# A decode backward pass on one core: the last dK tile is stored by GpSimd over fifteen DMA engines, the two small results by SyncE

## The chip, the cores and the metric

The kernel runs on one core of a Trainium2 chip. The metric is the device time of one execution in microseconds, the median of several. A core has the engines TensorE (PE, its weight loads PEld), VectorE (DVE), ScalarE (ACT), GpSimd (POOL) and SyncE (SP), and 16 DMA engines that move data between the memory of the chip and the core's on-chip memory of 128 partitions. SyncE, ScalarE and GpSimd can issue transfers, each into a queue of its own; the same 16 DMA engines serve all queues.

## What is computed

Attention with one query per head over a context of 8192, forward and backward: 32 heads of 128 elements, bf16.

```python
def _fwd_reference(q, k, v):          # q (1,32,1,128), k and v (1,32,8192,128)
    scale = q.shape[-1] ** -0.5
    scores = jnp.einsum('bhqd,bhkd->bhqk', q, k) * scale
    attn = _softmax(scores, axis=-1)
    return jnp.einsum('bhqk,bhkd->bhqd', attn, v)

def reference(q, k, v, grad_out):
    _out, _vjp = jax.vjp(_f, q, k, v)     # _f calls _fwd_reference
    _grads = _vjp(grad_out)
    return (out, dq, dk, dv)
```

The outputs out and dq are small, 32 rows of 128 elements each. dk and dv are as large as k and v: 67 MB each. So 134 MB are read and 134 MB written.

## The kernel before, in words

**Tiles.** The work goes through 16 tiles t of two heads (HP = 16). In a tile, partition p holds 128 consecutive rows of the two heads' 16384, that is 32 KB in one piece of K and as much of V (`rows_of`, L75). A whole tile of K or V is 4 MB. Three buffers hold K tiles and two hold V tiles.

**Stages of a tile.** K is transposed by VectorE and multiplied with q by TensorE (`k_block`, L184 and L192). The scores go through max, exp and sum. V is transposed by TensorE, copied by ScalarE (L253, L259) and multiplied with grad_out (`v_scores`, L270). From the softmax p and those products come ds, the gradient at the scores. `contract` (L309) sums p times V to out and ds times K to dq on TensorE. `outer` (L329, VectorE) forms dV = p times grad_out in place over V, and dK = ds times q in place over K, each in eight parts r of 16 columns. `store` (L339) sends dV and dK to memory.

**Order.** The order of instructions on each engine is that of the program text (`manual_schedule`). The loop runs t from 0 to 16; the dK of a tile is formed one round later, as tile o = t - 1. In the last round, t = 16, only the dK of tile 15 is left: `dk(0, 2)`, `dk(2, 3)`, `dk(3, 4)` and `dk(4, 8)`, that is eight products one after the other, with a store after every second one, because tile 15 is stored in four parts (`parts`). The dK of tile 14 is stored in two halves. The dV of tile 15 is stored in four quarters too (`fine`), the one before in one piece. A quarter is 1 MB: 32 of the 128 columns of every partition, in each partition one piece of 8 KB.

**Queues.** All large loads (`load`, L81) and all stores (`store`, L339) are issued by SyncE. ScalarE issues three small transfers in all: grad_out at the start, and in `results` (L341 to L351) the two result rows out and dq from `fin_sb`. GpSimd clears buffers in the first 5 us and issues no transfer. Each transfer counts on a semaphore when it has landed; there are fewer semaphores than transfers, so they are used again, and a transfer that uses one again is issued only after the earlier transfer on it has landed.

`do_cols` (128 partitions x 2 x 32, bf16) holds the columns of grad_out. It is written once at the start, and `weights_do` (L178) reads it, last for tile 15, at about 568 us. `Kt[t]` is the K buffer of tile t, where dK stands too.

Of the kernel before, what the change touches and what calls it, by code (L numbers as in the profile page):

```python
# [15 lines left out]
NB = 8  # L16
# [11 lines left out]
def kernel(  # L28
# [11 lines left out]
    nc = tc.nc  # L40
    P = 128
    _, H, S, D = k.shape
    HP = H // 2
    NT = 2 * S // P
# [27 lines left out]
    Kt = {t: k_in[t % K_BUFS] for t in range(HP)}  # L72
    Vt = {t: v_in[t % V_BUFS] for t in range(HP)}

    def rows_of(x, t, a, b):  # L75
        return x[0, 2 * t:2 * t + 2].rearrange("h s d -> (h s) d").rearrange("(p n) d -> p n d", p=P)[:, a:b, :]
# [70 lines left out]
    do_cols = consts.tile([P, 2, H], BF16)  # L147
# [33 lines left out]
    def k_block(t, c):  # L181
        x = st[t]
        X = xkpool.tile([P, BN, NW, QD], F32, tag="XK", name="XK_sb")
        nc.vector.transpose(X[:], Kt[t][:, c * BN:(c + 1) * BN, :].rearrange("p n d -> p (n d)").bitcast(F32).rearrange(  # L184
            "p (n w j) -> p n w j", n=BN, w=NW))
        if c == 0:
            x["s"] = psS.tile([P, 512], F32, tag="s", name="s_ps")
        cols = X[:].rearrange("p n w i -> p (n w i)").bitcast(BF16).rearrange(
            "p (n w i e) -> p w e n i", n=BN, w=NW, e=2)
        for w in range(NW):  # L190
            for e2 in range(2):
                nc.tensor.matmul(x["s"][:], lhsT=q_win[:, 2 * w + e2, SL - 1 - c:SL - 1 - c + P],  # L192
                                 rhs=cols[:, w, e2], start=(c == 0 and w == 0 and e2 == 0),
                                 stop=(c == NB - 1 and w == NW - 1 and e2 == 1), skip_group_check=True)

    def s_back(t):
        x = st[t]
        x["sT"] = backs.tile([P, BN, QD], F32, tag="back", name="sT")
        nc.vector.transpose(x["sT"][:].rearrange("p n r -> p (n r)"), x.pop("s")[:])  # L199

    def s_top(t):
        x = st[t]
        mx = small.tile([P, 1], F32, tag="mx")
        nc.vector.reduce_max(mx[:], x["sT"][:, :, 0:NB], axis=AX.XY)  # L204
        top = small.tile([P, 1], F32, tag="top")
        nc.vector.tensor_scalar_mul(top[:], mx[:], scale)
        nc.tensor.transpose(x["m"][:, 128:256], top[:].to_broadcast([P, P]), ident_f[:])  # L207

    def s_exp(t):
        x = st[t]  # L210
        nbias = small.tile([P, 1], F32, tag="nbias")
        for s in range(2):
            a, b = s * HF, (s + 1) * HF
            nc.vector.tensor_reduce(nbias[a:b], x["m"][a:b, 128 + a:128 + b], axis=AX.X, op=ALU.max, negate=True)
        e = x["e"] = single.tile([P, NT], F32, tag="e", name="e")
        rs = small.tile([P, 1], F32, tag="rs")
        nc.scalar.activation(e[:].rearrange("p (c n) -> p n c", c=NB), x["sT"][:, :, 0:NB], ACT.Exp, bias=nbias[:],
                             scale=scale, accum_out=rs[:])
        return rs
# [41 lines left out]
    def v_scores(t, z):  # L261
        x = st[t]
        cols = x.pop(("XV", z)).rearrange("p m s -> p (m s)").bitcast(BF16).rearrange(
            "p (m s e) -> p e m s", s=P, e=2)
        if z == 0:
            x["dp"] = psD.tile([P, 512], F32, tag="dp", name="dp_ps")
        at = SL - 2 - 2 * z
        for e2 in range(2):
            for b in range(NQ):
                nc.tensor.matmul(x["dp"][b * QD:(b + 1) * QD, :], lhsT=do_win[:, b // 2, e2, at:at + QD],  # L270
                                 rhs=cols[:, e2, :, b * QD:(b + 1) * QD],
                                 start=(z == 0 and e2 == 0), stop=(z == NZ - 1 and e2 == 1), skip_group_check=True)
# [52 lines left out]
    def outer(t, which, r):  # L325
        x = st[t]
        X, row = (Kt[t], 0) if which == "ds" else (Vt[t], 1)
        a, b = r * BN, (r + 1) * BN
        nc.vector.tensor_tensor(  # L329
            X[:, a:b, :].rearrange("p n (a b) -> p n a b", b=R),  # L330
            x[which][:, a:b, :].unsqueeze(2).to_broadcast([P, BN, D // R, R]),
            x["qd"][:, row, :].rearrange("p (a b) -> p a b", b=R).unsqueeze(1).to_broadcast([P, BN, D // R, R]),
            op=ALU.mult)

    def store(t, which, parts=1, last=None):
        X, dst = (Kt[t], out_2) if which == "ds" else (Vt[t], out_3)
        L = NT // parts
        for c in (range(parts) if last is None else (last,)):
            nc.sync.dma_start(rows_of(dst, t, c * L, (c + 1) * L), X[:, c * L:(c + 1) * L, :])  # L339

    def results():  # L341
        half = single.tile([P, 2, H], BF16, tag="ds1", name="half")
        nc.scalar.copy(half[:, 0], o_all[:])
        nc.scalar.copy(half[:, 1], dq_all[:])
        fin_ps = psT.tile([P, 2 * TB, P], BF16, tag="T", name="fin_ps")
        for i in range(2):
            nc.tensor.transpose(fin_ps[0:H, i, :], half[:, i], ident[:])
        fin_sb = small.tile([H, 2, D], BF16, tag="qd", name="fin_sb")
        nc.scalar.copy(fin_sb[:], fin_ps[0:H, 0:2, :])
        for i, dst in enumerate((out_0, out_1)):  # L350
            nc.scalar.dma_start(dst.rearrange("b h s d -> (b h s) d"), fin_sb[:, i])  # L351

    NV = NZ * NM // TB

    def v_part(t, m):
        v_bank(t, m)
        v_copy(t, m)
# [18 lines left out]
    for t in range(HP + 1):  # L376
        o = t - 1
        now, old = t < HP, t > 0
        parts = 4 if o == HP - 1 else 2 if o == HP - 2 else 1

        def dk(a, b):
            for r in range(a, b if old else a):
                outer(o, "ds", r)
                if (r + 1) % (NB // parts) == 0:
                    store(o, "ds", parts, r * parts // NB)

        dk(0, 2)
        if now:
            if old:
                v_part(t, 3)  # L390
                v_part(t, 4)
            s_back(t)
            s_top(t)
            if old:
                v_scores(t, 0)
                v_part(t, 5)
                v_part(t, 6)
        dk(2, 3)
        if now:
            rs = s_exp(t)  # L400
            if old:
                for m in (7, 8, 9):
                    v_bank(t, m)
            s_sum(t, rs)
            if old:
                v_copy(t, 7)
                v_copy(t, 8)
        dk(3, 4)
        if now:
            p_of(t)  # L410
            if old:
                v_copy(t, 9)
                v_scores(t, 1)
                v_part(t, 10)
                v_part(t, 11)
                contract(t, "p")
                v_part(t, 12)
                v_part(t, 13)
                v_scores(t, 2)
                v_part(t, 14)  # L420
                v_part(t, 15)
                v_scores(t, 3)
            else:
                contract(t, "p")
            if old and t + 1 < HP:
                weights_do(t + 1)
        dk(4, NB)
        if not now:
            break
        fine = t == 0 or t == HP - 1  # L430
        outer(t, "p", 0)
        outer(t, "p", 1)
        if fine:
            store(t, "p", 4, 0)
        v_back(t)
        pd_sum(t)
        if t % ST == 0 and old:
            gather(o, "ds")
        outer(t, "p", 2)
        ds_of(t)  # L440
        contract(t, "ds")
        if t % ST == ST - 1:
            gather(t, "p")
        if t + 1 < HP:
            prepare(t + 1)
        else:
            gather(t, "ds")
        for r in range(3, NB):
            outer(t, "p", r)
            if fine and r % 2:  # L450
                store(t, "p", 4, r // 2)
            if t + 1 < HP and t != 1 and r >= HALF - 1:
                k_block(t + 1, r - HALF + 1)
        if not fine:
            store(t, "p")
        if t == 1:
            for c in range(HALF + 1):
                k_block(t + 1, c)
        if t + 1 < HP:
            for c in range(HALF + 1, NB):  # L460
                k_block(t + 1, c)
                v_part(t + 1, c - HALF - 1)
            if t + 2 < HP:
                weights_q(t + 2)
        if 0 < t and t + 2 < HP:
            load_k(t + 2)
        if t + 2 < HP:
            load_v(t + 2, 4 if t == 0 else 1)
# [33 lines left out]
```

## Time and profile before

| what | value |
|---|---|
| median of 3 runs | 641.52 us (640.98 to 641.76) |
| the profiled execution's own time | 641.36 us |
| its span (first to last instruction) | 639.6 us |
| busy: PE, DVE, ACT, POOL | 450.8, 503.8, 195.8, 4.4 us |
| moved by DMA | 268.97 MB, mean 421 GB/s |
| of that in SyncE's queue (q1) | 268.45 MB in 12000 packets |
| of that in ScalarE's queue (q10) | 0.02 MB in 144 packets |
| dV of tile 15, four stores: issued from, median to landing | 606.78 us, 12.9 us |
| dK of tile 15, four stores: issued from, median to landing | 624.04 us, 9.8 us |
| fin_sb, two transfers: issued from, median to landing | 619.25 us, 5.0 us |

The profile is of one execution. A row of the windows gives, for a stretch of the span, each engine's busy time with its number of instructions, then the granted clock of TensorE, the mean busy share of the 16 DMA engines, and GB/s. A row of the waits gives who waited for what, the total, how often, and the longest. A row of the timeline gives start and length, engine, line, operation, and what it writes and reads; x4 means four instructions merged, and then the length runs from the first one's start to the last one's end. SPq and ACTq mark what an engine's sequencer does, such as issuing a transfer. The trace also has a record for each packet that a DMA engine moved: its start, its length, its bytes and its queue, but not which engine it was. Data packets here have 8, 16 or 32 KB, and a packet of 4 bytes counts the semaphore at the end of a transfer on each engine.

### The profile page before, as it was taken

How to read it: one execution, taken by the hardware profiler on the slowest of the kernel's cores; microseconds unless marked ns; L12 is line 12 of the kernel's file. 1: busy time of each engine (PE TensorE's matmuls, PEld its weight loads, DVE VectorE, ACT ScalarE, POOL GpSimd, SP SyncE). 2: the span in 40 equal slices, each digit the busy share in tenths (PEclk: the TensorE clock that was granted, in tenths of full speed). 3: DMA queues.
4: the chain of work that ended last, by engine and by line, in shares of the span. 5: the costliest groups of instructions: out<-in, count | busy, mean ns of one | idle time of the engine just before them, and what ended most of it. 6: DMA issues, size and time to landing. Idle time of an engine off the chain costs nothing.

```text
span 639.6 us, 8002 instructions
## 1 busy us (share of the span) xinstructions
PE 450.8 (70%) x3256; PEld 241.5 (38%) x3256; DVE 503.8 (79%) x608; ACT 195.8 (31%) x455; POOL 4.4 (1%) x10
## 2 busy tenths in 40 slices
PE   6668597778869387595875948759587584875840
PEld 5225253443525134162441614316244151431530
DVE  3788989979879598695977959778597795978990
ACT  6114334241605215052150602406124060240610
POOL 2000000000000000000000000000000000000000
PEclk9978788986969779696787978869588695887965
DMA  8999999999999999999999999999999999999986
GB/s 351 436 428 409 436 430 437 432 430 422 433 433 431 431 427 424 441 438 427 426 426 443 428 413 439 429 410 427 419 434 430 411 432 418 430 419 415 425 379 271
DMA packets 12180, 268.97 MB, mean 421 GB/s; under 512 B 1520, under 2 KB 1520, under 8 KB 1520
## 3 DMA queue, kind: packets, MB, share of 16 engines
q1 hardware_dynamic: 12000, 268.45, 98.6%
q8 instruction: 25, 0.41, 0.2%
q14 instruction: 11, 0.09, 0.0%
q10 hardware_dynamic: 144, 0.02, 0.0%
HBM read 134.23 MB, written 134.23 MB: 420 GB/s over the span
## 4 chain that ended last, share of the span: by engine, by line
DMA 40%; DVE 28%; PE 15%; issue 11%; ACT 4%; SPq 1%; DVEq 0%; ACTq 0%
DMA K<-in_k_dram 40%; DVE XK_sb L184 17%; PE s_ps L192 6%; PE T_ps L253 5%; DVE K L329 4%; DVE V L329 4%; ACT XV_sb L259 2%; PE dp_ps L270 2%; PE acc_p L309 1%; DVE sT L199 1%; ACT p_rep L235 0%; PE m_ps L207 0%; SPq L81 0%; DVE dpT L280 0%; DVE mx L204 0%
## 5 line engine op out<-in xcount | busy, mean ns | idle before, releaser
L192 PE MATMUL s_ps<-XK_sb,q_win 128*128 128x512 bf16 x512 | 173.2, 478 | 90.5 <-DVE XK_sb L184 89.8
L184 DVE STREAM_TRANSPOSE XK_sb<-K 128x1024 f32<-128x1024 f32 x128 | 152.6, 1223 | 85.8 <-DMA K<-in_k_dram 84.9
L259 ACT COPY XV_sb<-T_ps 128x512 f32<-128x512 f32 x240 | 130.3, 590 | 282.5 <-PE T_ps L253 282.1
L329 DVE TENSOR_TENSOR V<-p_rep,qd 128x2048 bf16<-128x2048 bf16 x128 | 151.9, 1202 | 2.0 <-PE acc_p L309 2.0
L329 DVE TENSOR_TENSOR K<-ds_rep,qd 128x2048 bf16<-128x2048 bf16 x128 | 149.9, 1214 | 0.5
L253 PE MATMUL T_ps<-ident_f,V 128*128 128x128 f32 x1024 | 136.9, 281 | 0.0
L253 PEld LDWEIGHTS T_ps<-ident_f,V 128*128 128x128 f32 x1024 | 116.1, 143 | 38.8 <-issue 11.4
L192 PEld LDWEIGHTS <-q_win 128*128 128x128 bf16 x512 | 57.8, 114 | 188.6 <-issue 166.4
L309 PE MATMUL acc_ds<-K,win_ds 128*32 128x512 bf16 x512 | 54.0, 596 | 27.8 <-ACT win_ds L228 27.8
L270 PE MATMUL dp_ps<-XV_sb,do_win 128*32 128x512 bf16 x480 | 37.2, 384 | 12.9 <-ACT XV_sb L259 11.9
L309 PEld LDWEIGHTS <-win_ds 128*32 128x32 bf16 x512 | 17.1, 132 | 51.6 <-ACT win_ds L228 27.2
L309 PE MATMUL acc_p<-V,win_p 128*32 128x512 bf16 x512 | 32.3, 396 | 3.7 <-ACT win_p L228 1.9
L170 ACT CAST qd<-m_ps 128x256 bf16<-128x256 f32 x16 | 6.0, 372 | 48.3 <-PE m_ps L166 48.2
L228 ACT COPY win_ds<-ds 64x128 bf16<-64x128 bf16 x32 | 9.5, 296 | 36.1 <-DVE ds L296 35.9
L309 PEld LDWEIGHTS <-win_p 128*32 128x32 bf16 x512 | 12.7, 99 | 18.6 <-ACT win_p L228 5.4
L289 PE MATMUL m_ps<-pd,same 128*128 128x1 f32 x32 | 6.1, 260 | 18.7 <-DVE m_ps L283 18.7
L270 PEld LDWEIGHTS <-do_win 128*32 128x32 bf16 x512 | 11.3, 94 | 20.0 <-issue 16.3
L280 DVE STREAM_TRANSPOSE dpT<-dp_ps 128x512 f32<-128x512 f32 x16 | 11.5, 717 | 4.8 <-PE dp_ps L270 4.8
L289 PEld LDWEIGHTS m_ps<-pd,same 128*128 128x128 f32 x32 | 4.8, 188 | 27.1 <-DVE m_ps L283 27.1
L199 DVE STREAM_TRANSPOSE sT<-s_ps 128x512 f32<-128x512 f32 x16 | 11.4, 711 | 4.4 <-PE s_ps L192 4.4
L233 DVE RECIPROCAL rinv<-m_ps 128x1 f32<-128x1 f32 x16 | 2.7, 168 | 14.2 <-PE m_ps L222 14.2
L235 ACT ACTIVATE p_rep<-e,rinv 128x512 bf16<-128x512 f32 x16 | 12.0, 747 | 0.9 <-DVE rinv L233 0.9
(61 smaller groups left out, 159.5 us busy)
## 6 DMA issues: line engine op xcount, KB each, us to landing
K<-in_k_dram SPq DMA_DIRECT2D x15, 4096.0 KB, 19.9
V<-in_v_dram SPq DMA_DIRECT2D x14, 4096.0 KB, 19.4
out_dram<-K SPq DMA_DIRECT2D x14, 4096.0 KB, 29.0
out_dram<-V SPq DMA_DIRECT2D x14, 4096.0 KB, 20.8
V<-in_v_dram SPq DMA_DIRECT2D x8, 1024.0 KB, 9.7
out_dram<-V SPq DMA_DIRECT2D x8, 1024.0 KB, 15.0
K<-in_k_dram SPq DMA_DIRECT2D x4, 1024.0 KB, 16.4
out_dram<-K SPq DMA_DIRECT2D x2, 2048.0 KB, 15.0
```

What stands on the lines that cost most here:

```text
L184: nc.vector.transpose(X[:], Kt[t][:, c * BN:(c + 1) * BN, :].rearrange("p n d -> p (n d)").bitcast(F32).rearrange("p (n w j) -> p n w j", ...
L192: nc.tensor.matmul(x["s"][:], lhsT=q_win[:, 2 * w + e2, SL - 1 - c:SL - 1 - c + P], rhs=cols[:, w, e2], start=(c == 0 and w == 0 and e2 == 0),
L199: nc.vector.transpose(x["sT"][:].rearrange("p n r -> p (n r)"), x.pop("s")[:])
L228: nc.scalar.copy(win[which][a:b, :, at + 4 * s:at + 4 * s + 4], src[a:b].rearrange("p (g j) -> p g j", j=4))
L235: nc.scalar.activation(x["p"][:], x["e"][:].unsqueeze(2).to_broadcast([P, NT, R]), ACT.Copy, scale=rinv[:])
L253: nc.tensor.transpose(T_ps[:, j, :], words[:, at * P:(at + 1) * P], ident_f[:])
L259: nc.scalar.copy(x["XV", z][:, i * TB:(i + 1) * TB, :], x.pop(("T", m))[:])
L270: nc.tensor.matmul(x["dp"][b * QD:(b + 1) * QD, :], lhsT=do_win[:, b // 2, e2, at:at + QD], rhs=cols[:, e2, :, b * QD:(b + 1) * QD], start ...
L280: nc.vector.transpose(dpT[:].rearrange("p m r -> p (m r)"), x.pop("dp")[:])
L289: nc.tensor.matmul(x["m"][:, 1:2], lhsT=same[:], rhs=x["pd"][:], start=True, stop=True, skip_group_check=True)
L309: nc.tensor.matmul(acc[which][b * QD:(b + 1) * QD, :], lhsT=win[which][:, g, at:at + QD], rhs=X[:, 4 * g:4 * g + 4, :].rearrange("p n d -> ...
L329: nc.vector.tensor_tensor(X[:, a:b, :].rearrange("p n (a b) -> p n a b", b=R), x[which][:, a:b, :].unsqueeze(2).to_broadcast([P, BN, D // ...
```

## The change

The dK of tile 15 is no longer stored by SyncE in four quarters of 128 partitions. GpSimd issues four quarters of partitions 0 to 119 (15 times 8), each after its two products as before, and after the fourth one transfer of partitions 120 to 127 with all 128 columns, 32 KB in each. Before, between and after these GpSimd issues loads of a few elements of q into columns of `do_cols` that nobody reads any more (`turn`): one of 5 rows after the loop over the dV products of tile 15, one of 17 rows after each quarter, one of 3 rows at the end. Each row is two elements of 2 bytes that do not lie side by side in q. These loads serve only to move on the place in the cycle of DMA engines at which GpSimd's next transfer begins. The argument `max_dma_last_dim` keeps a row of 8 KB, or 32 KB, in one piece. The transfers of `fin_sb` are issued by SyncE and no longer by ScalarE. Nothing else changes: same products, same bytes of results.

```diff
+    def turn(n, at):
+        nc.gpsimd.dma_start(do_cols[0:n, 0, 2 * at:2 * at + 2].unsqueeze(2), q[0, 0:n].rearrange("h s d -> (h s) d")[
+            :, 0:4].rearrange("h (a b) -> h a b", b=2)[:, :, 0:1])
+
+    def store_spread(t, c):
+        L = NT // 4
+        nc.gpsimd.dma_start(rows_of(out_2, t, c * L, (c + 1) * L)[0:120], Kt[t][0:120, c * L:(c + 1) * L, :],
+                            max_dma_last_dim=L * D)
+        turn(17, c + 1)
+        if c == 3:
+            nc.gpsimd.dma_start(rows_of(out_2, t, 0, NT)[120:P], Kt[t][120:P], max_dma_last_dim=NT * D)
+            turn(3, c + 2)
+
     def results():
...
         for i, dst in enumerate((out_0, out_1)):
-            nc.scalar.dma_start(dst.rearrange("b h s d -> (b h s) d"), fin_sb[:, i])
+            nc.sync.dma_start(dst.rearrange("b h s d -> (b h s) d"), fin_sb[:, i])
...
                 if (r + 1) % (NB // parts) == 0:
-                    store(o, "ds", parts, r * parts // NB)
+                    if o == HP - 1:
+                        store_spread(o, r // 2)
+                    else:
+                        store(o, "ds", parts, r * parts // NB)
...
+        if t == HP - 1:
+            turn(5, 0)
         if not fine:
             store(t, "p")
```

## The prediction

> **What bounds the kernel now.** I read four views: the page's slices and queues, a table by windows over the last 20 us, SyncE's waits, and the timeline of the end.
>
> ```profile
> DMA  8999999999999999999999999999999999999986
> GB/s 351 436 428 409 436 430 437 432 430 422 433 433 431 431 427 424 441 438 427 426 426 443 428 413 439 429 410 427 419 434 430 411 432 418 430 419 415 425 379 271
> ...
> q1 hardware_dynamic: 12000, 268.45, 98.6%
> ```
>
> The 16 DMA engines are full from the second slice to the 38th, nearly all of it in SyncE's queue (q1). VectorE is next, busy for 79% of the span. So an edit at the end pays only if it removes DMA idleness. The page's chain of waits stops at the last dK product of VectorE (625 us) and does not show the last 15 us; the windows do (columns: PE, PEld, DVE, ACT, POOL busy and counts, clock, DMA share, GB/s).
>
> ```profile
> 620.00:621.00 1.00, 0.00 (x0) 0.00 (x0) 1.00 (x2) 0.00 (x0) 0.00 (x0) 0.50 0.99 413
> 621.00:622.00 1.00, 0.00 (x0) 0.00 (x0) 1.00 (x2) 0.00 (x0) 0.00 (x0) 0.50 0.57 234
> 622.00:623.00 1.00, 0.00 (x0) 0.00 (x0) 1.00 (x2) 0.00 (x0) 0.00 (x0) 0.50 0.39 160
> 623.00:624.00 1.00, 0.00 (x0) 0.00 (x0) 1.00 (x2) 0.00 (x0) 0.00 (x0) 0.50 0.14 53
> 624.00:625.00 1.00, 0.00 (x0) 0.00 (x0) 0.97 (x1) 0.00 (x0) 0.00 (x0) 0.50 0.33 140
> 625.00:630.00 5.00, 0.00 (x0) 0.00 (x0) 0.00 (x0) 0.00 (x0) 0.00 (x0) 0.50 1.00 415
> ...
> 636.00:637.00 1.00, 0.00 (x0) 0.00 (x0) 0.00 (x0) 0.00 (x0) 0.00 (x0) 0.50 0.06 25
> 637.00:638.00 1.00, 0.00 (x0) 0.00 (x0) 0.00 (x0) 0.00 (x0) 0.00 (x0) 0.50 0.08 33
> ```
>
> There are two holes. From 621 to 625 us the shares missing from 1 add up to 0.43 + 0.61 + 0.86 + 0.67 = 2.57 us of all engines. From 635 us on the share is one sixteenth: one engine works alone.
>
> The trace's packet records say who. On one engine each packet begins as the one before ends, and a transfer is eight data packets and one of 4 bytes; so each engine's packets can be chained back from its last. An 8 KB packet takes 0.309 us, a 32 KB one 1.213, and a quarter (eight of 8 KB) 2.45 us. Fifteen engines end the last dV quarter between 620.6 and 623.9 us, stand still until 624.9, and end the last dK quarter at 634.9. The sixteenth, S from here on, ends dV at 628.4, never stops, and ends dK at 638.24. It has been last in every transfer for 100 us: its 4 MB transfers take 9.7 to 10.2 us, those of others 9.68.
>
> ```profile
> SPq L497 <- DMA out_dram<-K: 10.7, 4, 3.5
> SPq L339 <- DMA out_dram<-fin_sb: 8.3, 2, 7.7
> ```
>
> ```profile
> 615.80 9.17 DVE L329 TENSOR_TENSOR K<-ds_rep,qd 128x2048 bf16<-128x2048 bf16 x8
> ...
> 619.25 1.15 ACTq L351 DMA_DIRECT2D out_dram<-fin_sb  x2
> 624.04 3.84 SPq L339 DMA_DIRECT2D out_dram<-K  x4
> ```
>
> The first hole's cause stands here. The first dK quarter is computed at 618.1 us (two of the eight products), but SyncE issues it at 624.04, as the first result row lands. In the landing records the first two dK quarters count on the semaphores of the two fin_sb transfers, so they wait for them, and those wait in turn among S's packets.
>
> **The change, part by part.** All against the profiled execution: 641.36 us, span 639.57, and 1.79 around it. The median, 641.52, is 0.16 above.
>
> 1. Four SyncE issues of dK go, and with them the wait of 7.7 us. GpSimd, idle since 5 us, issues instead as each pair of products ends: 618.1, 620.4, 622.7 and 625.0. What is late next is each engine's own dV rest, not the issue.
>
> 2. From issue to first packet SyncE needs 0.83 us (624.04 to 624.87). GpSimd's price is not in this trace: at the low end SyncE's 0.83 us; at the high end a start only when VectorE is done, 625.0. I take 1.5 us a quarter, nearer to the issue rows (0.33 to 1.22 us long) than to the other end. Then the quarters can start at 619.6, 621.9, 624.2 and 626.5. The earliest engine needs them at 620.6, 623.1, 625.5 and 628.0, the latest, which sets the end, 3.3 us later. So this costs nothing; the cover is 1 us on the earliest and about 4.6 us on the latest engine.
>
> 3. S, if it is the engine left out, loses four quarters (9.8 us of packets) and is done at 628.4. The other fifteen keep eight rows a quarter (120 = 15 x 8), as many as now.
>
> 4. The last 8 rows add one 32 KB packet, 1.21 us, to eight engines behind their fourth quarter. The latest engine then ends at 623.93 + 4 x 2.45 + 1.21 = 634.95 us if it is one of the eight, 633.74 if not; the next (623.4) ends 0.5 us earlier. I take 634.95.
>
> 5. Six tiny loads of 34, 10 or 6 elements: the nearest rows are packets of 4 B (9 ns) and 256 B (15 to 18 ns), so 34 take 0.3 us. On a full engine each can also wait for one 8 KB packet, as the fin_sb packets on S did: 34 x 0.318 = 10.8 us, from 618.4 to 629.2 at worst. They add only the 0.3 us to that engine's own work, and nothing but the end, at 634, waits for their landing. Cost 0.
>
> 6. The result rows move from ScalarE's queue to SyncE's, behind the four dV issues; SyncE is free from 616.3, fin_sb is ready at 619.2, so they issue when they do now (0.33 to 0.77 us each) and land about 5 us later, near 625. No store stands behind them any more. Cost 0.
>
> 7. Last landing to end is 0.88 us now (638.69 to 639.57). There are more transfers to wait for; SyncE's satisfied waits at the end stand 0.06 us apart, so up to eight more cost at most 0.5. I take 0.2.
>
> Sum: the last packet ends 638.24 - 634.95 = 3.29 us earlier, less 0.2: 3.1 us. Span 636.5, execution 638.3, median **638.4 us**.
>
> **The rivals.**
>
> *The engine left out is not S.* The trace does not number the engines, so the aim of the turned cursor can't be tested on it; this is the change not doing what it says. S then has 628.4 + 9.8 = 638.2, plus 1.21 if it also gets one of the eight rows, and filling the first hole does nothing for it since S was never idle. That gives 641.7 to 642.9 us. For it: nothing here says which engine S is. Against: with S hit, the sum holds. The Trainium skill (DMA: Bandwidth & Descriptors, Why a DMA increments its semaphore) has GpSimd's shares go to consecutive engines from a round-robin cursor, which from a cursor at 0 and a turn of five would leave out engine 4; the same page (Latency and other measured facts) calls engines 7 and 15 the usually slower ones. If S is one of those, that is this rival; the traces show one slow engine and no number.
>
> *Late descriptors.* If GpSimd's issues come through only once VectorE stops at 625.0, the quarters start near 625.8 on all engines and the end is 625.8 + 9.8 + 1.2 = 636.9, a gain of 1.2 us with the 0.2 above: 640.3. At 4.6 us and more for each quarter with its tiny load, nothing is left: 641.5. Against it: GpSimd shows no work after 5 us. I take 640.3 to 641.5.
>
> *Slower: engines that share a way out of SBUF.* With 128 rows over 16 engines all packets run at the same 27 GB/s (32 KB in 1.213 us), each engine with rows of its own. With 120 rows over 15 the assignment is another, and pairs of engines may draw on the same rows' path; two at once would each take up to 2 x 0.309 us a packet. With a stretch f of the dK part the end is 623.93 + 9.8 f + 1.21 against 638.24: it decides from f = 1.33. At f = 1.5, two engines in step half the time, the end is 639.85 and the median 643.3; at f = 2 it is 644.8 and the median 648.2. For it: the lags (0 to 3.3 us) are about a quarter's length, so the engines are not spread by design. Against it: no row shows that a path carries no more than one engine's 27 GB/s, and no packet of the last stretch took longer than its neighbours. The middle is 645.7. The Trainium skill (SBUF — State Buffer, Door 1: the DMA port swizzle) states such paths: partitions 32 apart lie on the same port, and partitions 0 to 63 gave hardly more than 0 to 31, 196 against 189 GB/s. By that rule shares of eight neighbouring rows collide in pairs, and the last eight rows lie on two ports, so that their 1.21 us would become 4.85; no transfer of this trace shows it.
>
> **How the numbers follow.** S left out and all else streaming: 0.57 (637.2 to 639.6). Not S: 0.14. Late descriptors: 0.10. Shared paths: 0.19. That S is hit is my choice, not a reading: the edit steers which engine is spared, and I give the miss one chance in four against the hit. 0.2% of the median is 1.28 us, about what a measurement of this kernel can tell from no change, so the bounds are 640.24 and 642.80. Faster: 0.57 and 0.02 of the late descriptors, 0.59. Same: 0.08 of these and 0.10 of the miss, 0.18. Slower: 0.19 and 0.04 of the miss, 0.23. The range takes in the first three cases: 637.2 to 643.3. The likeliest case's own range is 637.2 to 639.6: below by the latest engine without one of the eight rows (1.2 us), above by 0.5 us of waits and 0.7 us of slower issue.
>
> **What would show it.** Right: no hole at 621 to 625 us in the DMA share; the first dK packets by 620 us; no stretch of one sixteenth at the end but a fall within 2 us; the last landing near 635.4. Wrong: one engine alone to 638 us (not S); share near 1 but 8 KB packets of 0.4 us and more (shared paths); POOL issues of more than 3 us or dK packets only after 625 (descriptors). The prediction falls most easily with step 3, the identity of the engine left out.

## The result, and the profile after

| | before | after |
|---|---|---|
| median, us | 641.55 (640.95 to 642.37, 6 runs) | 646.21 (644.38 to 646.46, 6 runs) |
| profiled execution, us | 641.36 | 646.17 |
| its span, us | 639.57 | 644.40 |
| last data packet ends, us | 638.24 | 642.47 |
| dK of tile 15: four quarters, median from issue to landing, us | 9.8 | 15.2 |

The change makes the kernel slower: the ratio of after to before is 1.0069 [1.0055, 1.0082], 4.7 us. The forecast was 638.4 us, its range ended at 643.3.

The page of the kernel after, the same slices and queues as before:

```profile
DMA  8999999999999999999999999999999999999995
GB/s 355 434 442 390 438 436 428 431 431 432 428 433 427 429 436 425 439 422 438 427 433 437 423 410 437 424 425 431 423 435 428 409 423 417 420 430 420 423 373 153
...
q1 hardware_dynamic: 11520, 264.27, 96.3%
q0 software_dynamic: 1328, 4.20, 2.2%
```

Here is the pitfall of this case. The DMA row looks better than before: no slice is below 9 but the first and the last. The GB/s row below it says 373 in slice 39, where it was 379, and 153 in slice 40, where it was 271. An engine counts as busy while a packet is on its way, however slowly. GpSimd's queue is q0.

The last 22 us by windows (columns as before: five engines, clock, DMA share, GB/s), kernel after:

```profile
620.00:622.00 2.00, 0.00 (x0) 0.00 (x0) 2.00 (x3) 0.00 (x0) 1.45 (x3) 0.50 0.98 389
622.00:624.00 2.00, 0.00 (x0) 0.00 (x0) 2.00 (x3) 0.00 (x0) 1.43 (x2) 0.50 0.99 302
624.00:626.00 2.00, 0.00 (x0) 0.00 (x0) 1.47 (x2) 0.00 (x0) 1.43 (x3) 0.50 1.01 276
626.00:628.00 2.00, 0.00 (x0) 0.00 (x0) 0.00 (x0) 0.00 (x0) 1.47 (x2) 0.50 1.01 320
...
632.00:634.00 2.00, 0.00 (x0) 0.00 (x0) 0.00 (x0) 0.00 (x0) 0.55 (x1) 0.50 0.90 310
634.00:636.00 2.00, 0.00 (x0) 0.00 (x0) 0.00 (x0) 0.00 (x0) 0.60 (x2) 0.50 0.84 192
636.00:638.00 2.00, 0.00 (x0) 0.00 (x0) 0.00 (x0) 0.00 (x0) 0.00 (x0) 0.50 0.33 78
638.00:640.00 2.00, 0.00 (x0) 0.00 (x0) 0.00 (x0) 0.00 (x0) 0.00 (x0) 0.50 0.11 29
640.00:642.00 2.00, 0.00 (x0) 0.00 (x0) 0.00 (x0) 0.00 (x0) 0.00 (x0) 0.50 0.08 31
```

The hole of 621 to 625 us is gone, the share is 1. But it carries 276 to 320 GB/s; before, a share of 1 carried 415. And the tail of one engine at 25 to 31 GB/s is still there, now to 642.

The packet records say the same in another way. `max_dma_last_dim` did not keep a row in one piece: a row of 8 KB went as two packets of 4 KB, a row of 32 KB as two of 16 KB. A 4 KB packet alone takes 0.159 us. From 622 to 632 us their mean is 0.19 to 0.23 us and the longest 0.73. S has no dK packet: at the end one engine has only the last dV rows and packets of 4 bytes. Yet of its last sixteen dV packets, 0.309 us each before, nine now take 0.66 to 1.22 us, and its dV ends at 635.2 us instead of 628.4. The engine that ends last is another: its third quarter ends at 638.6, its fourth at 641.15, and two packets of 16 KB bring it to 642.47.

SyncE's waits in the last 45 us, and then GpSimd's, kernel after:

```profile
SPq L517 <- DMA out_dram<-K: 21.4, 1, 21.4
```

```profile
POOL out_dram L349 <- DVE K L329: 612.3, 4, 610.6
POOL out_dram L353 <- DMA out_dram<-K: 6.0, 1, 6.0
```

SyncE's wait of 7.7 us for fin_sb is gone; it only waits for the end (L517). GpSimd waits for its data (612.3 us, nearly all before the first quarter), and for one thing that the prediction did not have: the store of the last 8 rows (L353) stands 6.0 us until the first dK quarter has landed, since it counts on the same semaphore. Fifteen of that quarter's sixteen counts are in by 627.41 us, the last comes at 633.17. The records point to S, the engine without data: from 625 to 633 us each dV packet of S is followed by one packet of 4 bytes from GpSimd's queue (at 626.14, 628.52 and 632.84 us, for example) before its next dV packet, and S has sixteen of those a quarter to get through. The timeline of GpSimd's issues gives the places:

```profile
618.97 0.75 POOL L349 DMA_DIRECT2D out_dram<-K  x1 [610.61 <-DVE K L329]
...
625.77 0.74 POOL L349 DMA_DIRECT2D out_dram<-K  x1 [0.57 <-DVE K L329]
626.50 0.96 POOL L344 DMA_DIRECT2D do_cols<-in_q_dram  x1
633.45 0.58 POOL L353 DMA_DIRECT2D out_dram<-K  x1 [5.99 <-DMA out_dram<-K]
```

### The profile page after: what moved, and what is told of

It reads as the page before. It is cut to its first block, busy times and chain, and to the rows that moved or that the text cites. A ratio compares the mean times of both kernels' runs of the same rounds, so it can differ in the third digit from the quotient of the medians.

```text
span 644.4 us, 8013 instructions
## 1 busy us (share of the span) xinstructions
PE 442.0 (69%) x3256; PEld 237.4 (37%) x3256; DVE 503.5 (78%) x608; ACT 195.8 (30%) x455; POOL 13.1 (2%) x21
## 4 chain that ended last, share of the span: by engine, by line
DMA 41%; DVE 29%; PE 14%; issue 11%; ACT 4%; POOL 0%; DVEq 0%; POOLq 0%; ACTq 0%; SPq 0%
DMA K<-in_k_dram 34%; DVE XK_sb L184 17%; DMA out_dram<-K 7%; PE T_ps L253 6%; DVE K L329 4%; DVE V L329 4%; PE s_ps L192 3%; PE dp_ps L270 2%; ACT XV_sb L259 2%; PE acc_p L309 1%; DVE sT L199 1%; PE m_ps L207 1%; ACT p_rep L235 1%; DVE mx L204 1%; DVE dpT L280 1%
## 5 line engine op out<-in xcount | busy, mean ns | idle before, releaser
L192 PE MATMUL s_ps<-XK_sb,q_win 128*128 128x512 bf16 x512 | 168.2, 464 | 96.9 <-DVE XK_sb L184 95.8
L349 POOL DMA_DIRECT2D out_dram<-K x4 | 3.0, 742 | 612.3 <-DVE K L329 612.3
L199 DVE STREAM_TRANSPOSE sT<-s_ps 128x512 f32<-128x512 f32 x16 | 11.4, 710 | 2.3 <-PE s_ps L192 2.3
```

## Experiments

The theory after the result: **shared ways.** 120 rows in fifteen shares put two engines on one way out of SBUF (the on-chip memory), and both slow down. The rivals: GpSimd's own queue is slow (small packets, descriptors, tiny loads); the wrong engine is left out; the last 8 rows with their wait are the whole loss. Each ratio below is against the kernel before as measured beside it.

### e1_gpsimd_128: GpSimd's queue with all 128 rows

```diff
+    def store_spread(t, c):
+        L = NT // 4
+        nc.gpsimd.dma_start(rows_of(out_2, t, c * L, (c + 1) * L), Kt[t][:, c * L:(c + 1) * L, :],
+                            max_dma_last_dim=L * D)
```

No tiny loads and no transfer of 8 rows; the results go by SyncE as in the change.

> GpSimd stores the last dK in four quarters of all 128 rows, without tiny loads and without the extra 8-row transfer; results in SyncE's queue as in the change. Theory 'shared ways out' (eight neighbouring rows per engine make pairs of engines read over one way): with 128 rows each engine has its own rows again, packets keep 0.159 us per 4 KB, the slow engine S is the last at about 638.2 us of the span as before, median 641.3 to 642.3. Rival 'software queue' (GpSimd's transfers of 4 KB packets are slow in themselves): packets stretch as in the change, median 644 to 647. Rival 'late 8 rows': also 641 to 642 here, so this run does not tell it from the theory.

Measured: 641.89 us, ratio 1.0007 [0.9997, 1.0016]. Two windows of it, one in the full stretch and one in the tail:

```profile
624.00:626.00 2.00, 0.00 (x0) 0.00 (x0) 1.58 (x2) 0.00 (x0) 0.45 (x2) 0.50 1.03 413
...
634.00:636.00 2.00, 0.00 (x0) 0.00 (x0) 0.00 (x0) 0.00 (x0) 0.00 (x0) 0.50 0.06 27
```

The same queue, the same packets of 4 KB, issued behind the same products: 413 GB/s where the change had 276.

| window, us | after: 4 KB packet, mean and longest, ns | e1: the same |
|---|---|---|
| 622 to 624 | 229, 691 | 160, 198 |
| 624 to 626 | 208, 728 | 162, 234 |
| 628 to 630 | 193, 626 | 163, 259 |
| 632 to 634 | 174, 536 | 159, 159 |

So GpSimd's queue and its small packets are not the cause; the tiny loads, which are missing here too, are settled by e4. Fifteen engines end by 634 us, and S alone goes on to 638.79, as before.

### e2_results_sync: only the results move to SyncE, dK as before

```diff
-            nc.scalar.dma_start(dst.rearrange("b h s d -> (b h s) d"), fin_sb[:, i])
+            nc.sync.dma_start(dst.rearrange("b h s d -> (b h s) d"), fin_sb[:, i])
```

> The kernel before with one edit: the two result transfers are issued by SyncE after the dV quarters. Theory (S is never idle in the last 100 us, so S alone sets the end): the hole at 621 to 625 us closes for fifteen engines, S still ends at 638.2, median 641.2 to 641.8, no change. Rival (the hole is what costs): 2.6 us less, 638.7 to 639.3.

Measured: 641.91 us, ratio 1.0011 [1.0002, 1.0021]. Three windows:

```profile
622.00:624.00 2.00, 0.00 (x0) 0.00 (x0) 2.00 (x2) 0.00 (x0) 0.00 (x0) 0.50 1.00 422
...
630.00:632.00 2.00, 0.00 (x0) 0.00 (x0) 0.00 (x0) 0.00 (x0) 0.00 (x0) 0.50 0.59 240
...
636.00:638.00 2.00, 0.00 (x0) 0.00 (x0) 0.00 (x0) 0.00 (x0) 0.00 (x0) 0.50 0.06 25
```

The hole of 2.57 us is filled, 422 GB/s where it was 106 in the same two microseconds, and S still ends at 638.31 (638.24 before). Closing the hole is worth nothing; the whole gain of the forecast had to come from S.

### e3_halves: another way to collide, without GpSimd

```diff
+        for s in range(2):
+            nc.sync.dma_start(rows_of(out_2, t, c * L, (c + 1) * L)[s * HF:(s + 1) * HF],
+                              Kt[t][s * HF:(s + 1) * HF, c * L:(c + 1) * L, :])
```

e2, with each dK quarter stored by SyncE as partitions 0 to 63 and 64 to 127 (HF = 64).

> As the run with results in SyncE's queue, but each of the last four dK quarters is two SyncE transfers, partitions 0 to 63 and 64 to 127, four neighbouring rows on each of 16 engines; same bytes, same 8 KB pieces, same number of packets, no GpSimd. Theory 'shared ways out': engines j and j+8 read over one way, 8 KB packets of 0.31 us become up to 0.62 us, dK takes up to 20 us and not 10; median 644 to 651. Rival 'software queue': no GpSimd, so no stretch, 641 to 642. Rival 'late 8 rows': 641 to 642.

Measured: 645.75 us, ratio 1.0075 [1.0059, 1.0092]. Two windows:

```profile
626.00:628.00 2.00, 0.00 (x0) 0.00 (x0) 0.00 (x0) 0.00 (x0) 0.00 (x0) 0.50 0.92 225
628.00:630.00 2.00, 0.00 (x0) 0.00 (x0) 0.00 (x0) 0.00 (x0) 0.00 (x0) 0.50 0.79 193
```

All 16 engines, SyncE's own queue, no small loads: the 8 KB packets take 0.36 to 0.56 us in the mean of the windows from 620 to 636 us, and the rate from 622 to 632 us is 248 GB/s, where e1 has 405. It is the set of rows in one transfer that makes the packets slow. The Trainium skill (SBUF — State Buffer, Door 1: the DMA port swizzle) states 196 GB/s for partitions 0 to 63, since they reach eight of sixteen ports; the slowest window here, 193, is near it. The other windows from 622 to 636 us have 221 to 307, so the trace comes to that figure only at its lowest.

### e4_sync_120: the change's row split, all by SyncE

```diff
+        nc.sync.dma_start(rows_of(out_2, t, c * L, (c + 1) * L)[0:120], Kt[t][0:120, c * L:(c + 1) * L, :],
+                            max_dma_last_dim=L * D)
+        if c == 3:
+            nc.sync.dma_start(rows_of(out_2, t, 0, NT)[120:P], Kt[t][120:P], max_dma_last_dim=NT * D)
```

> The row shares of the change (four times 120 rows, then 8 rows of 32 KB), all issued by SyncE, no tiny loads. Theory 'shared ways out': packets stretch as in the change, and if SyncE spares another engine than S, S carries its dK too: median 645 to 652. Rival 'software queue': packets of 0.31 us, median 641 to 643. Rival 'late 8 rows' (the wait of 6 us on a semaphore set the end): no such wait here, 641 to 643.

Measured: 649.94 us, ratio 1.0137 [1.0120, 1.0154]. Two windows:

```profile
624.00:626.00 2.00, 0.00 (x0) 0.00 (x0) 1.16 (x2) 0.00 (x0) 0.00 (x0) 0.50 0.90 293
...
640.00:642.00 2.00, 0.00 (x0) 0.00 (x0) 0.00 (x0) 0.00 (x0) 0.00 (x0) 0.50 0.06 25
```

The rate is 293 to 354 GB/s from 622 to 632 us, the 4 KB packets have means of 0.17 to 0.22 us, and from 640 us on one engine works alone at 25 to 27 GB/s until 646.03. The row split slows the packets whoever issues it, and without any tiny load. Here one engine has dK packets to the end, and the tail is 3.6 us longer than after's (642.47).

### e5_no_8_rows: the change without its last 8 rows

```diff
         if c == 3:
-            nc.gpsimd.dma_start(rows_of(out_2, t, 0, NT)[120:P], Kt[t][120:P], max_dma_last_dim=NT * D)
-            turn(3, c + 2)
+            turn(11, c + 2)
```

The lines are against the change. Partitions 120 to 127 of the last dK are not stored.

> The changed kernel without the last transfer of 8 rows (partitions 120 to 127 of the last dK are not stored; the last tiny load has 11 rows so that the cursor comes round). Theory 'shared ways out': the four quarters themselves are stretched, the last engine ends them near 640, median 643 to 645.5, that is 1 to 3 us below the change. Rival 'late 8 rows' (its wait of 6 us and its own 8 us set the end): all of the loss goes, 639 to 641.5.

Measured: 645.18 us (643.18 to 645.85), ratio 1.0050 [1.0032, 1.0067]. The last 8 rows and their wait are worth about 1.0 us of the 4.7 by the medians (the intervals of the two ratios overlap a little); some 3.7 us stay with the four quarters alone.

### e6_spare_next: the next engine is left out

```diff
-            turn(3, c + 2)
+            turn(2, c + 2)
...
-            turn(5, 0)
+            turn(6, 0)
```

> The changed kernel with the first tiny load of 6 rows and the last of 2, so that the next engine is left out of the last dK and no longer the one that the change leaves out. If the change left out S (theory): S now carries its dK after a dV that is itself stretched to 630 or later, and ends near 645 or later, median 647 to 655. Rival 'wrong engine spared' (S was not left out in the change): no more than 1 us from the change, or faster, 638 to 647.

Measured: 648.53 us, ratio 1.0107 [1.0092, 1.0123]; the last packet ends at 644.45. One engine lands its last dV quarter at 638.2 us, 9 us behind all others, and one engine alone has dK packets to the end: S carries dK again. So the change had hit S, and missing it costs 2.3 us more.

### e7_relief_13 and e8_relief_odd: relief earlier, by SyncE's share of dK

If the fifteen must not collide at the end, S might be relieved earlier. Both build on e2. In e7 the first dK quarter of tile 13 goes by GpSimd (120 rows, from 556 us), the rest by SyncE; e8 does so in all odd tiles from 1 to 13.

```diff
+    RELIEF = (13,)                      # e8: (1, 3, 5, 7, 9, 11, 13)
...
+            nc.gpsimd.dma_start(rows_of(out_2, t, 0, L)[0:120], Kt[t][0:120, 0:L, :], max_dma_last_dim=L * D)
...
+            nc.sync.dma_start(rows_of(out_2, t, L, NT), Kt[t][:, L:NT, :])
+            nc.sync.dma_start(rows_of(out_2, t, 0, L)[120:P], Kt[t][120:P, 0:L, :])
```

> The kernel with results in SyncE's queue, and S relieved earlier: of dK of tile 13 the first quarter of columns is stored by GpSimd, 120 rows over the fifteen engines without S, while the engines load tile 15; the other 8 rows and the other columns go by SyncE as usual. Theory (each row has one way out, S is late by its own work): while the engines load, that way is free, so S saves 2.45 us and ends near 636, the others stay near 634; median 639 to 640.3. Rival (any 120-row transfer costs more than it saves): 641.5 to 644.

Measured: 641.47 us, ratio 0.9996 [0.9987, 1.0006]: nothing. The records show why the place was wrong. While these packets went (560.7 to 580.9 us), S was still storing the dV of tile 13, whose last count came at 570.91 us; in e2 it came at 569.27. SyncE's next V load waits for that. Its wait in e7, and then in e2:

```profile
SPq L81 <- DMA out_dram<-V: 11.0, 1, 11.0
```

```profile
SPq L81 <- DMA out_dram<-V: 9.8, 1, 9.8
```

The load was issued at 570.98 us, 11.4 us after the K load before it, where e2 has 10.2. S ended at 638.20.

> As the run that relieves S in tile 13, but in tiles 1, 3, 5, 7, 9, 11 and 13. Theory (S alone is slower by 1.2 us a tile and paces the whole kernel): 2.45 us saved in every second tile takes most of that lag away, median 628 to 637. Rival (S paces only the end, the middle is bound by the loads of all engines or by the order of work): 639 to 642. Rival (120-row transfers cost more than they save): over 643.

Measured: 650.26 us, ratio 1.0157 [1.0104, 1.0210]. The idea that relief of S helps anywhere falls with it: 8.7 us lost over seven tiles, 1.2 us a tile, about as much as the V load was late in e7. That this late load is what each tile loses is argued from e7, not measured in e8. Whether S paces the middle of the kernel stays open: in e2 fifteen engines have landed the dV of tile 13 by 564.04 us, and the V load is issued only after S, at 569.33.

### e10_relief_dv14, e11_relief_split and e12_relief_two: relief while S loads

e2, and the first quarter of the dV of tile 14 by GpSimd, issued at 568.31 us in e10, ahead of the V load of tile 15 (issued at 570.32), so that its packets (572.2 to 591.0 us) run for the most part while S loads. e11 also splits that V load into four parts. e12 adds the first dK quarter of tile 13, behind the dV quarter in GpSimd's queue. SyncE stores the rest of these tiles as in e7.

```diff
+    def first_quarter(t, which):
+        X, dst = (Kt[t], out_2) if which == "ds" else (Vt[t], out_3)
+        L = NT // 4
+        nc.gpsimd.dma_start(rows_of(dst, t, 0, L)[0:120], X[0:120, 0:L, :], max_dma_last_dim=L * D)
...
+        if t == HP - 2:
+            turn(5, 0)
+            first_quarter(t, "p")
+            turn(17, 1)                        # e12 only
+            first_quarter(o, "ds")             # e12 only
+            turn(12, 2)
...
-            load_v(t + 2, 4 if t == 0 else 1)
+            load_v(t + 2, 4 if t in (0, HP - 3) else 1)     # e11 and e12
```

> The kernel with results in SyncE's queue; of dV of tile 14 the first quarter of columns goes by GpSimd from about 568 us, 120 rows over the fifteen engines without S, the rest by SyncE. S loads tile 15 from about 569 to 588 us, so nothing of its own leaves its rows then. Theory 'shared ways out, and free while S loads': S saves up to 2.45 us and no load waits for a store that is stretched; S ends near 636.3, median 639.2 to 640.8. Rival (a 120-row transfer costs as much as it saves wherever it lies): 641.3 to 643.

> As the run with dV of tile 14, and the load of V of tile 15 in four parts, so that its packets are 8 KB and not 32 KB and GpSimd's 4 KB packets get turns more often: the quarter is out by about 580 us. Theory: all of it leaves while S loads, S saves 2.45 us, median 638.8 to 640.3. Rival: 641.3 to 643.

> As the run with the load in four parts, and also the first quarter of dK of tile 13 by GpSimd, behind the other. Theory: S saves 4.9 us and ends near 634, where the other engines end too; median 637 to 639.5. Rival: stretched packets of the two quarters and of the stores beside them cost more than S saves, 641.3 to 644.

| | median, us | ratio | S's last packet ends, us |
|---|---|---|---|
| e10 | 639.76 | 0.9969 [0.9958, 0.9981] | 637.23 |
| e11 | 640.51 | 0.9982 [0.9973, 0.9991] | 636.37 |
| e12 | 638.64 | 0.9952 [0.9937, 0.9967] | 635.23 |

All three are faster than both kernels, by 0.2 to 0.5% against the kernel before. The medians of e10 and e12 lie in the theory's ranges, that of e11 0.2 us above its own. e10 and e11 can't be told apart by their ratios. The end of e12:

```profile
630.00:632.00 2.00, 0.00 (x0) 0.00 (x0) 0.00 (x0) 0.00 (x0) 0.00 (x0) 0.50 0.87 361
632.00:634.00 2.00, 0.00 (x0) 0.00 (x0) 0.00 (x0) 0.00 (x0) 0.00 (x0) 0.50 0.26 105
634.00:636.00 2.00, 0.00 (x0) 0.00 (x0) 0.00 (x0) 0.00 (x0) 0.00 (x0) 0.50 0.06 22
```

The others now end later than in e2 (0.87 at 630 to 632 us, where e2 had 0.59) and S earlier, 635.23 against 638.31: the work was moved from S to them. It is the same row split that lost at the end. The difference is in the packets: of GpSimd's 4 KB packets 19% took over 0.2 us in the change, 3.5% in e12 (the longest 1.03), and 0.6% in e1 with all 128 rows. In e12 they run among loads and whole-tile stores, in the change all engines with data only store. That this is why fewer are slow is argued, not shown.

## Why the prediction was wrong

By its own steps:

1. *The wait goes, the hole closes*: right. The share is 0.98 to 1.03 from 620 to 630 us, no wait for fin_sb is left.
2. *1.5 us from issue to first packet, at no cost*: the size was off, the conclusion held. The issue took 0.75 us and the first dK packet ran at 621.2, 2.2 us after the issue at 618.97. e1, with GpSimd's issues within 0.2 us of the same times, ended as e2 did, so it cost nothing.
3. *S is the engine left out*: right, and it was the step that I called the weakest. After's records show one engine without dK, and e6 lost 2.3 us by missing it. The other half of the step, that S is done at 628.4 us, was wrong: its dV went on to 635.2, though it was not the last engine even so.
4. **The failed step: "The other fifteen keep eight rows a quarter (120 = 15 x 8), as many as now", priced at 2.45 us a quarter** (end of step 3, summed in step 4). The amount is right, the rate is not. Counted from 623.93, where the sum had its dV end, the latest engine needed 641.15 - 623.93 = 17.2 us for four quarters where the sum had 9.8: a stretch of 1.76 in the terms of the slower rival, which decides from 1.33 and whose middle, 1.75, gave 645.7 us. Its fourth quarter took 2.55 us, nearly as priced; the stretch lies before it. The sign that the prediction had named for this rival came too: a share near 1, with S's 8 KB packets far over 0.4 us. Over all engines the rate from 622 to 632 us was 308 GB/s against 405 in e1, a mean stretch of 1.3; the latest engine had more than the mean, and it sets the end. The runs bear out the rival's mechanism as far as this: equal queue and packets with 128 rows run undisturbed (e1), row subsets stretch without GpSimd (e3, e4). The Trainium skill (DMA: Bandwidth & Descriptors, The descriptor swizzle) has a transfer of 128 partitions give each engine the rows of one port of its own; e1's 405 to 413 GB/s from 622 to 630 us fits that. That rows 32 apart share a way was not measured by itself.

   Of the last 8 rows, 1.21 us were right only for the latest engine, which had them to itself by then (1.3 us). The other fourteen packets of 16 KB, 0.611 us when undisturbed, took 0.6 to 3.2 us. Together they lasted from 634.8 to 639.9 us, 5.1 us where the sum had 1.21 and the slower rival named 4.85. And they could not start before 633.45 for the wait on the semaphore, a term that the prediction did not have. e5 puts the whole of that at about 1.0 us.
5. *Tiny loads*: cost 0, right to about 0.2 us. GpSimd issues one of 17 rows in 0.96 us, and they land 14.6 us after their issue (the worst case was put at 10.8), but only SyncE's last wait sees them (1.3 us, for do_cols); the last one lands at 643.12 us, 0.2 behind the last dK. In e12 three of them stand in a faster kernel.
6. *Results on SyncE*: cost 0, right by e2, which is 0.7 us slower by its median, within 0.2%. The landing was wrong: not 5 us after the issue, near 625, but 17.0, at 635.5 and 635.7, behind S's dV. Nothing waited for it.

```profile
out_dram<-fin_sb SPq DMA_DIRECT2D x2, 8.0 KB, 17.0
```

7. *Last landing to end*: the sum had 1.55 us from the last packet to the end of the span, measured 644.40 - 642.47 = 1.93.

The span missed by 7.9 us (644.40 for 636.5): 7.5 in the last packet (642.47 for 634.95) and 0.4 behind it. Two judgments stand behind it. The prediction named the slower rival and its mechanism, but gave it 0.19, and took "no packet of the last stretch took longer than its neighbours" as evidence against shared ways, although every large transfer there had 128 rows and could not have shown one. And the gain asked that S's dV go on at its old pace while other engines store dK. In the trace after, S's own dV packets stretch to 1.22 us while the others store dK, and S's dV ends 6.8 us later: moving dK from S's queue did not take it out of S's way.

What stays open: why S is slower than the others, and why e11's median stands above e10's although its S ends earlier in the profile. Where the engines meet is open as well: every transfer compared is a store, which reads SBUF and writes the chip's memory, so no run tells a shared way out of SBUF from one into that memory. Two engines taking turns would double a packet's time; packets of four and five times are not explained by a pair alone. That e10 and e12 gain because S's rows have room while S loads fits the packet times, but no run moved the same quarter through the same stretch without S's load in it.

## What to carry to other kernels

A DMA share of 1 says that packets are under way, not that bytes move; read the GB/s row and the packet times beside it before work is moved to "free" engines. A transfer of a part of the partitions (120 in fifteen shares, or 64 in sixteen) ran at 193 to 354 GB/s in the windows from 622 to 632 us, where one of all 128 had 405 to 434 while all engines had work, so sparing one slow engine at the end cost more than its tail. If one engine is always last, take work from it earlier, while it loads (e12: 0.9952), and test each place, since the same edit one transfer earlier gave nothing (e7) and in seven tiles lost 1.6% (e8).

## What the runs showed of the hardware that was not expected

- Transfers that carry `max_dma_last_dim` ran in packets of as many bytes as the number given: 4096 for rows of 8 KB (960 packets for 480 rows) and 16384 for rows of 32 KB, issued by GpSimd or by SyncE (e4). SyncE's stores without it kept 8 KB and 32 KB, also for 8 rows alone (e7). So the argument, and not GpSimd's queue, is the likely cause; no GpSimd store without it was run.
- A transfer on fewer engines still puts packets on the others: 16 of 4 bytes a quarter on the engine left out, and 136 bytes (34 elements of 4) on each engine without data of a tiny load. The 4-byte ones take turns with the packets of the other queue, one after each dV packet of S, and the first quarter counted as landed only at 633.17 us, 5.8 us after fifteen engines were through.
- GpSimd issued the first tiny load at 7.66 us, 608 us ahead of its place behind the last dV products: before it, it waited only 2.7 us for ScalarE's copy from do_cols. The engine left out was S all the same.
- Single packets of the row split took up to five times as long as undisturbed ones: 16 KB in 3.16 us against 0.611, 4 KB in 0.73 against 0.159.
